# Earlier turns and first products of the next unit, and seven block products in another order

## The chip, the cores and the metric

The kernel runs on one core of a Trainium2 chip. What counts is the device time of one execution in microseconds; the times before are from ten runs. A core has TensorE (PE, with its weight loads PEld), VectorE (DVE), ScalarE (ACT), GpSimd (POOL) and SyncE (SP), which here issues the transfers. Each engine works through its own queue in the order of the program.

## The reference

A recurrent attention (RWKV-6) over 4 x 8 sequences of 768 tokens with 48 channels per head, and behind it a gated two-layer network.

```python
# attention: r, k, v, w are [4, 8, 768, 48], u is [8, 48]
for t in range(S):
    kt, vt, rt, wt = (k[:, :, t], v[:, :, t], r[:, :, t], w[:, :, t])
    cur = np.einsum('bhd,bhe->bhde', u[None] * kt, vt)
    y[:, :, t] = np.einsum('bhd,bhde->bhe', rt, state + cur)
    state = wt[:, :, :, None] * state + np.einsum('bhd,bhe->bhde', kt, vt)
# network: x = y as [3072, 384], w_in [384, 2048], w_out [2048, 384]
h = x @ w_in
g = h * (1.0 / (1.0 + np.exp(-h)))
out = g @ w_out
```

## The kernel before, in words

The work is cut into twelve units, numbered 0 to 11: a unit is a chunk of 128 tokens of two batches (256 tokens, 8 heads each). Units 0 and 1 load by tokens, units 2 to 11 by blocks of 32. For a unit the attention has these steps.

- `turn` (L360, VectorE) transposes the raw blocks of w, k and r, two instructions each. `product` (L408, GpSimd) builds a tree of products of the decays w, level by level, seven in all. `grow_own` multiplies keys (L634, GpSimd) and queries (L607, VectorE) by decays for levels 0 and 1; `odd_keys` (L595, ScalarE), `grow_keys` (L625, GpSimd), `grow_queries` (L607) and `prepare` (L737) go on with the higher levels.
- `burst` has TensorE compute the scores of two levels (L669), and `keep_level` writes them under a mask into the score tile (L679, VectorE).
- The blocks of eight tokens nearest to the diagonal are computed apart: `block_bonus` (L487, GpSimd, steps 0 to 7), `block_sum` (L521, VectorE, steps 0 to 4), `block_move` (two transfers through `kept`), `block_spread` (L548 to L551, ScalarE and one shuffle) and `block_write` (L557, VectorE).
- `turn_k` transposes the keys on TensorE (L781); `y_state`, `y` (L794, L807) give the output of the attention, `update` (L821, L826 on GpSimd, L835 on VectorE) the new state, and `move_x` sends the output to the network's layout (L857, SP).

The network follows one and two units behind. While `mix(i)` runs the attention of unit i, TensorE also does the eight `up` steps of unit i-1 (L924, each with a gate L933 on ScalarE) and the second layer of unit i-2. That second layer is a 2 x 2 block product in seven multiplications instead of eight (Winograd's form): `sums` (L972, VectorE) makes four combinations s1 to s4 of the gated values in `quarters` (part of `temps`), `weight_sums` (L964, once) makes t1, t2, t3 and a new b12 of the weights, and `quarter(i, which)` runs one of the seven products (L990) into one of two PSUM buffers `p_o`; ScalarE (L997) or VectorE (L999) combines and evicts it. This document counts the products from 0 in the order in which they run.

The order of everything is written out by hand (`manual_schedule`): `mix` returns thirteen groups of steps, and after each group `ROOM` says how many steps of the network follow:

```python
ROOM = 1, 1, 1, 2, 2, 1, 1, 1, 2, 1, 1, 1, 0
steps = downs(i - 2) + ups(i - 1)
```

So the seven products stand among groups 0 to 4 and the eight `up` steps among groups 5 to 11. Before the change, groups 0 to 2 hold the turns of unit i, all products of the tree and `grow_own`; the first block bonus of unit i+1 stands in group 10, and its sums 0 and 1 and bonus 4 and 5 at the end of group 12. A tile that is allocated again (`tk`, `tw` once, `tr` and `p_o` twice) waits for the last reader of the buffer it takes.

Of the kernel before, what the change touches and what calls it, by code (L numbers as in the profile page):

```python
# [15 lines left out]
ALU = mybir.AluOpType  # L16
# [22 lines left out]
def kernel(  # L39
# [11 lines left out]
    nc = tc.nc  # L51
# [4 lines left out]
    NL = 7  # L56
    NB = 2
# [8 lines left out]
    units = [(n, b0) for n in range(S // L) for b0 in range(0, B, NB)]  # L66
    NSLOT = 2
    NTOK = 2
    NPAIR = 3
# [75 lines left out]
    second = []  # L145
# [177 lines left out]
    first = {}  # L323
# [10 lines left out]
    for b in range(NB):  # L334
        for x in range(2):
            nc.vector.tensor_single_scalar(out=own_mask[:, b, :, x:x + 1], in_=first[0], scalar=tok[:, x, b:b + 1],
                                           op=ALU.is_equal)
# [113 lines left out]
    at = 768  # L451
# [94 lines left out]
    def block_spread(i):  # L546
        flat = block_both.rearrange("p b h s -> p b (h s)")
        nc.scalar.copy(out=flat[:, 0], in_=block_diag[0])  # L548
        for g in range(4):
            nc.scalar.copy(out=flat[(3 - g) * 32:(4 - g) * 32, 1], in_=block_diag[1][g * 32:(g + 1) * 32])  # L550
        nc.vector.stream_shuffle(out=flat[:, 1], in_=flat[:, 1], mask=list(range(31, -1, -1)))  # L551

    def block_write(i):

        shape = [128, NB, NP, L // BLK, BLK]
        for e in range(2):
            nc.vector.copy_predicated(out=score[:, i % NSC, e].rearrange("p (b q) (i s) -> p b q i s", b=NB, s=BLK),  # L557
                                      mask=block_mask[:, :, None].to_broadcast(shape),
                                      data=block_both[:, :, e::2][:, :, :, None, :].to_broadcast(shape))
# [301 lines left out]
    def both(fn, i, *args):  # L861
        return [(fn, i, b, *args) for b in range(NB)]
# [3 lines left out]

    def mix(i):

        early = i > NPAIR
        ahead = i + 1 < len(units)  # L870

        def bonus_steps(*steps):
            return [(block_bonus, i, x) for x in steps]

        def sum_steps(*steps):
            return [(block_sum, i, x) for x in steps]

        next_bonus = [(block_bonus, i + 1, x) for x in range(4)] if ahead else []
        next_sums = [(block_sum, i + 1, 0), (block_sum, i + 1, 1), (block_bonus, i + 1, 4), (block_bonus, i + 1, 5)] if ahead and early else []
        late = i == NPAIR + 1  # L880
        next_load = [(load_rk, i + 1)] if ahead else []
        move = [*sum_steps(3, 4), (block_move, i), *next_load]
        placed = [(block_spread, i), (block_write, i)]
        first = not early

        def at(now, *steps):
            return steps if now else ()

        groups = [[*both(turn, i, "w"), (product, i, 0)],
                  [*both(turn, i, "k"), *both(turn, i, "r"), (grow_own, i, 0)],  # L890
                  [*[(product, i, l) for l in range(1, NL)], (grow_own, i, 1), *at(late, *sum_steps(0, 1))],
                  [(odd_keys, i, 2), (grow_keys, i, 2, False), (grow_queries, i, 2), *at(early and not late, *sum_steps(2))],
                  [(prepare, i, 3), *at(first, *bonus_steps(2, 3), *sum_steps(0)), *at(late, *bonus_steps(4, 5)),
                   *at(early and not late, *bonus_steps(6, 7))],
                  [(burst, i, 3), (keep_level, i, 3), *at(first, *sum_steps(1), *bonus_steps(4, 5)),
                   *at(late, *sum_steps(2), *bonus_steps(6, 7)), *at(early and not late, *move)],
                  [(keep_level, i, 4), (go_on, i, 4), *at(first, (make_block_mask,), *sum_steps(2), *bonus_steps(6)), *at(late, *move)],
                  [(prepare, i, 5), (reverse_v, i), *at(first, *bonus_steps(7))],
                  [*at(first, *move), *at(early, *placed)],
                  [(burst, i, 5), (keep_level, i, 5), (keep_level, i, 6), (go_on, i, 6)],  # L900
                  [*at(first, *placed), *next_bonus],
                  both(turn_k, i) if i < len(units) - NB else [],
                  [*both(y_state, i), *both(y, i), *both(update, i), *next_sums, (move_x, i)]]

        loads = block_loads(i + NSLOT) if i + NSLOT < len(units) else []
        if i + 1 < len(units):
            loads.insert(len(loads) // 2, (load_values, i + 1))

        behind = groups[3 if i > NTOK + 1 else 10:]
        for at, group in enumerate(behind):  # L910
            group += loads[at * len(loads) // len(behind):(at + 1) * len(loads) // len(behind)]
        return groups
# [3 lines left out]
    FH, DH = FC // 2, DM // 2  # L916
# [46 lines left out]
        out, one, two = ((t1, b12, b11), (t2, b22, t1), (t3, b22, b12), (b12, b21, t2))[which]  # L963
        nc.vector.tensor_tensor(out=out, in0=one, in1=two, op=ALU.subtract)  # L964

    def sums(i, m):

        lower, upper = (gt[i, x].rearrange("p a (b t) -> p b a t", b=NB) for x in (m, m + FH // 2))
        s1, s2, s3, s4 = (quarters[:, x, 2 * m:2 * m + 2, :] for x in range(4))
        for out, one, two, op in ((s1, lower[:, 1], upper[:, 1], ALU.add), (s2, s1, lower[:, 0], ALU.subtract),  # L970
                                  (s3, lower[:, 0], lower[:, 1], ALU.subtract), (s4, upper[:, 0], s2, ALU.subtract)):
            nc.vector.tensor_tensor(out=out, in0=one, in1=two, op=op)  # L972

    ob, partial = {}, {}
# [1 line left out]
    def quarter(i, which):  # L976

        n, b0 = units[i]

        def g(b, half):  # L980
            return lambda f: gt[i, (f + half * FH) // 2][:, f % 2, b * L:(b + 1) * L]

        def s(x):
            return lambda f: quarters[:, x, f, :]

        p = second[0].tile([128, DH], F32, name="p_o", bufs=2)

        left, right = ((g(0, 0), b11), (g(0, 1), b21), (s(1), t2), (s(2), t3), (s(0), t1), (g(1, 1), b12), (s(3), b22))[which]
        for f in range(FH):
            nc.tensor.matmul(p, lhsT=left(f), rhs=right[:, f, :], start=(f == 0), stop=(f == FH - 1))  # L990
        if which == 0:
            ob[i] = [out_room(b) for b in range(NB)]
            partial[i] = pt.tile([128, 4, DH], F32, name="partial", bufs=1)
        c11, c12, c21, c22 = (ob[i][x][:, y * DH:(y + 1) * DH] for x in range(2) for y in range(2))
        u1, u2, u3, u4 = (partial[i][:, x, :] for x in range(4))
        if which == 0:
            nc.scalar.copy(out=u1, in_=p)  # L997
        for to, known in ((), ((c11, u1),), ((u2, u1),), ((u3, u2),), ((c22, u3), (u4, u2)), ((c21, u3),), ((c12, u4),))[which]:
            nc.vector.tensor_tensor(out=to, in0=p, in1=known, op=ALU.add)  # L999
        if which >= 5:  # L1000
            b = 6 - which
            row0 = (b0 + b) * S + n * L
            nc.sync.dma_start(out=out[row0:row0 + L, :], in_=ob[i][b])

    def ups(i):

        steps = [[(up, i, m)] for m in range(FC // 2)]
        for m in range(FH // 2 - 1):

            steps[FH // 2 + 1 + m].append((sums, i, m))  # L1010
        steps[-1].append((sums, i, FH // 2 - 1))
        return steps

    def downs(i):
        return [[(quarter, i, x)] for x in range(7)]

    def do(*steps):
        for fn, *args in steps:
            fn(*args)
# [16 lines left out]
    blocks = block_loads(2)  # L1036
# [37 lines left out]
    for m in range(6):  # L1074
# [3 lines left out]

    blocks = block_loads(4)
    do(*blocks[0:2], (level, 2, 2), (prepare, 2, 3), (weight_sums, 1), (down, 0, 1, 0), (down, 0, 0, 3), (down, 0, 1, 1),  # L1080
       (sums, 1, 0), (bonus, 2, 0), (bonus_sum, 2, 0))
    do(blocks[2], (burst, 2, 3), (keep_level, 2, 3), (keep_level, 2, 4), (go_on, 2, 4), (prepare, 2, 5), (bonus, 2, 1),
       (bonus, 2, 2), (down, 0, 1, 2), (bonus_sum, 2, 1), (load_rk, 3), (load_u,), (sums, 1, 1), *blocks[3:7], (down, 0, 1, 3))
    do((burst, 2, 5), (keep_level, 2, 5), (keep_level, 2, 6), (go_on, 2, 6), (up, 1, 6), (bonus_spread, 2), (bonus_write, 2),
       (load_values, 3), *both(turn_k, 2), (weight_sums, 2), (up, 1, 7), (sums, 1, 2))
    do((sums, 1, 3), *both(y_state, 2), *both(y, 2), *both(update, 2),
       (block_bonus, 3, 0), (block_bonus, 3, 1), (move_x, 2),
       *blocks[7:])

    ROOM = 1, 1, 1, 2, 2, 1, 1, 1, 2, 1, 1, 1, 0  # L1090
# [1 line left out]
    for i in range(3, len(units)):  # L1092
        steps = downs(i - 2) + ups(i - 1)
        groups = mix(i)
        if i == NTOK + 1:

            groups[3].insert(0, (weight_sums, 3))
        for group, room in zip(groups, ROOM):
            do(*group)
            for step in steps[:room]:  # L1100
                do(*step)
            steps = steps[room:]
# [32 lines left out]
```

## Time and profile before

| | |
|---|---|
| median of 10 runs | 636.53 us (635.84 to 637.32) |
| profiled execution, its own time | 638.04 us |
| its span | 636.3 us |
| TensorE busy | 621.5 us, 98% |
| VectorE busy | 438.7 us, 69% |
| GpSimd busy | 371.0 us, 58% |
| ScalarE busy | 185.4 us, 29% |
| granted TensorE clock, mean | 0.995 |

Busy time is the sum over instructions; a share near 100% means that the engine's queue is the limit, if its instructions are not themselves stretched. A line of a timeline holds the start and the length in us, the engine, the source line, the operation, the tiles written and read, the shape, how many such instructions follow each other, and in brackets the idle time of the engine just before and what ended it. The products of unit i-2 stand at the head of the stage of unit i: they start at 128.2 us for i = 3, 184.7 for i = 4, 235.8 for i = 5, then at 286.5, 335.2, 383.9, 432.7, 481.4 and 528.5 for i = 6 to 11.

### The profile page before, as it was taken

How to read it: one execution, taken by the hardware profiler on the slowest of the kernel's cores; microseconds unless marked ns; L12 is line 12 of the kernel's file. 1: busy time of each engine (PE TensorE's matmuls, PEld its weight loads, DVE VectorE, ACT ScalarE, POOL GpSimd, SP SyncE). 2: the span in 40 equal slices, each digit the busy share in tenths (PEclk: the TensorE clock that was granted, in tenths of full speed). 3: DMA queues.
4: the chain of work that ended last, by engine and by line, in shares of the span. 5: the costliest groups of instructions: out<-in, count | busy, mean ns of one | idle time of the engine just before them, and what ended most of it. 6: DMA issues, size and time to landing. Idle time of an engine off the chain costs nothing.

```text
span 636.3 us, 12245 instructions
## 1 busy us (share of the span) xinstructions
PE 621.5 (98%) x4574; PEld 563.7 (89%) x4574; DVE 438.7 (69%) x750; ACT 185.4 (29%) x377; POOL 371.0 (58%) x421
## 2 busy tenths in 40 slices
PE   8999999979998998999999999999999999999997
PEld 7878876869898898889889989989989989989997
DVE  7879779895696597587578488588578676561031
ACT  5798881200220320320320320320231221220120
POOL 6998297578369558657557657647747747600000
PEclk9999999988999999999999999999999999999999
DMA  9965854543343552643453552453353222100000
GB/s 229 286 178 134 196 163 50 113 75 66 77 73 55 98 95 51 126 62 52 97 77 51 111 75 50 92 92 53 72 104 54 43 67 51 35 0 26 26 1 25
DMA packets 203291, 53.75 MB, mean 84 GB/s; under 512 B 186464, under 2 KB 194656, under 8 KB 203232
## 3 DMA queue, kind: packets, MB, share of 16 engines
q1 hardware_dynamic: 201648, 52.39, 40.4%
q10 hardware_dynamic: 1584, 0.59, 0.4%
q8 instruction: 36, 0.59, 0.4%
q14 instruction: 23, 0.19, 0.1%
HBM read 43.67 MB, written 5.31 MB: 77 GB/s over the span
## 4 chain that ended last, share of the span: by engine, by line
PE 79%; SPq 6%; DVE 5%; DMA 5%; POOL 2%; issue 2%; ACT 1%; POOLq 0%; DVEq 0%; ACTq 0%
PE p_h L924 31%; PE p_o L990 29%; PE p_sc L669 5%; SPq L109 4%; DMA tokens_w<-in_w_dram 3%; PE p_m L946 2%; PE p_m L807 2%; PE p_m L669 2%; PE p_m L794 2%; PE p_m L372 2%; POOL tk L625 1%; DVE score L679 1%; PE p_m L1025 1%; PE p_m L781 1%; DVE tw L360 1%
## 5 line engine op out<-in xcount | busy, mean ns | idle before, releaser
L924 PE MATMUL p_h<-xt,w_in_sb 128*128 128x256 f32 x1152 | 258.1, 382 | 0.7 <-DVE xt L847 0.7
L924 PEld LDWEIGHTS p_h<-xt,w_in_sb 128*128 128x128 f32 x1152 | 215.9, 190 | 32.6 <-POOL tk L649 0.9
L933 ACT ACTIVATE gt<-p_h 128x512 f32<-128x512 f32 x90 | 53.6, 597 | 227.6 <-PE p_h L924 227.5
L625 POOL TENSOR_TENSOR tk<-tk,tw 128x256 f32<-128x256 f32 x126 | 86.9, 711 | 33.8 <-ACT tk L595 14.6
L990 PE MATMUL p_o<-own,temps 128*128 128x192 f32 x528 | 91.2, 333 | 8.3 <-DVE temps L999 8.3
L990 PEld LDWEIGHTS p_o<-own,temps 128*128 128x128 f32 x528 | 88.8, 195 | 9.2 <-DVE temps L999 9.2
L487 POOL TENSOR_TENSOR ruk<-tokens_rk 128x768 f32<-128x768 f32 (+1 forms) x36 | 51.9, 1453 | 71.8 <-DVE block_sums L521 31.8
L990 PE MATMUL p_o<-w_out_sb,gt 128*128 128x192 f32 x508 | 87.3, 328 | 0.0
L990 PEld LDWEIGHTS p_o<-w_out_sb,gt 128*128 128x128 f32 x508 | 82.6, 190 | 0.9 <-issue 0.4
L972 DVE TENSOR_TENSOR temps<-gt 128x256 f32<-128x256 f32 x84 | 51.7, 615 | 28.7 <-ACT gt L933 28.6
L607 DVE TENSOR_TENSOR tr<-tr,tw 128x512 f32<-128x512 f32 x62 | 51.7, 834 | 13.1 <-POOL tw L408 10.0
L595 ACT COPY tk<-tk 128x256 f32<-128x256 f32 x51 | 20.5, 402 | 127.2 <-POOL tk L634 103.6
L408 POOL TENSOR_TENSOR tw<-tw 128x256 f32<-128x256 f32 (+6 forms) x83 | 47.6, 573 | 14.1 <-DVE tw L360 10.2
L679 DVE COPY_PREDICATED score<-mask,p_sc 128x512 f32<-128x512 int8 x60 | 42.1, 756 | 15.2 <-PE p_sc L669 14.4
L826 POOL TENSOR_TENSOR state<-state,tw 128x512 f32<-128x512 f32 x16 | 19.9, 1263 | 41.4 <-PE p_m L794 41.4
L669 PEld LDWEIGHTS p_sc<-tr,tk 48*128 48x128 f32 x496 | 30.4, 187 | 10.2 <-issue 6.3
L669 PE MATMUL p_sc<-tr,tk 48*128 48x128 f32 x496 | 36.5, 285 | 0.8 <-POOL tk L625 0.6
L557 DVE COPY_PREDICATED score<-spare 128x1024 f32<-128x1024 int8 x18 | 32.9, 1882 | 0.3
L999 DVE TENSOR_TENSOR temps<-p_o,partial 128x192 f32<-128x192 f32 x22 | 7.9, 358 | 36.0 <-PE p_o L990 25.8
L634 POOL TENSOR_TENSOR tk<-tk,tw 128x256 f32<-128x256 f32 x36 | 31.2, 888 | 0.0
L990 PE MATMUL p_o<-w_out_sb,temps 128*128 128x192 f32 x176 | 30.4, 326 | 0.0
L990 PEld LDWEIGHTS p_o<-w_out_sb,temps 128*128 128x128 f32 x176 | 28.9, 190 | 0.0
(170 smaller groups left out, 809.7 us busy)
## 6 DMA issues: line engine op xcount, KB each, us to landing
w_out_sb<-in_moe_w_in_dram SPq DMA_DIRECT2D x6, 768.0 KB, 6.7
tokens_rk<-in_r_dram SPq DMA_DIRECT2D x9, 384.0 KB, 4.4
tokens_rk<-in_k_dram SPq DMA_DIRECT2D x9, 384.0 KB, 5.3
tokens_w<-in_w_dram SPq DMA_DIRECT2D x9, 384.0 KB, 6.4
w_out_sb<-in_moe_w_out_dram SPq DMA_DIRECT2D x4, 768.0 KB, 6.7
own<-in_moe_w_out_dram SPq DMA_DIRECT2D x4, 768.0 KB, 6.2
xt<-yt SPq DMA_DIRECT2D x60, 48.0 KB, 2.0
raw<-in_w_dram SPq DMA_DIRECT2D x80, 32.0 KB, 2.2
```

The lines of the kernel that those rows point to most:

```text
L408: engine.tensor_tensor(out=up, in0=t[:, :, 0::2], in1=t[:, :, 1::2], op=ALU.mult)
L487: mul = lambda out, one, two: nc.gpsimd.tensor_tensor(out=out, in0=one, in1=two, op=ALU.mult)
L557: nc.vector.copy_predicated(out=score[:, i % NSC, e].rearrange("p (b q) (i s) -> p b q i s", b=NB, s=BLK), mask=block_mask[:, :, None].to_ ...
L607: nc.vector.tensor_tensor(out=odd, in0=odd, in1=tw[i][l][:, :, 0::2][:, :, :, None].to_broadcast([128, Q, L >> (l + 1), c]), op=ALU.mult)
L625: nc.gpsimd.tensor_tensor(out=out, in0=have, in1=odd_products(i, l, b, *blocks), op=ALU.mult)
L634: nc.gpsimd.tensor_tensor(out=have, in0=have, in1=odd_products(i, l, b, [2, NP * ni]), op=ALU.mult)
L669: nc.tensor.matmul(bass.AP(tensor=s_p.tensor, offset=s_p.offset, ap=[s_p.ap[0], [apart * L // 2, 2], [1, L // 2]]), lhsT=tk[i][rows, X[l % ...
L679: nc.vector.copy_predicated(out=dst, mask=masks[l][:, :, None].to_broadcast([128, NB, NP, ni, c]), data=sc[e].rearrange("p (b q) (i c) -> ...
L924: nc.tensor.matmul(p_h[:, a, :], lhsT=w_in_sb[:, c, f * 128:(f + 1) * 128], rhs=xt[i][:, c, :], start=(c == 0), stop=(c == KC - 1))
L933: nc.scalar.activation(out=gt[i, m], in_=p_h, func=AF.Silu)
L972: nc.vector.tensor_tensor(out=out, in0=one, in1=two, op=op)
L990: nc.tensor.matmul(p, lhsT=left(f), rhs=right[:, f, :], start=(f == 0), stop=(f == FH - 1))
```

## The change

It has three parts. First, from unit 4 on the turns, the tree and `grow_own` of unit i+1 are issued at the end of unit i: the turns, the first product of the tree and `grow_own` of level 0 between `turn_k` and `y_state`, the rest behind `update`. Unit 3, the first to run in `mix`, keeps them at its head. Secondly, the block steps of units 3, 4 and 5 stand at other places: unit 3 does its bonus steps 0 to 3 in group 4, unit 4's bonus steps 0 to 3 stand at the end of unit 3 and its sums 0 and 1 and bonus 4 and 5 in group 2, and the last shuffle of `block_spread` goes into `block_write`. Thirdly, the seven products run in another order, and s4 and s3 are computed between them: s4 behind product 1, s3 behind product 2. `weight_sums(2)` moves into group 2 of unit 3, `weight_sums(3)` to the end of its group 3.

```diff
 def block_spread(i):
...
-        nc.vector.stream_shuffle(out=flat[:, 1], in_=flat[:, 1], mask=list(range(31, -1, -1)))
 def block_write(i):
+        flat = block_both.rearrange("p b h s -> p b (h s)")
+        nc.vector.stream_shuffle(out=flat[:, 1], in_=flat[:, 1], mask=list(range(31, -1, -1)))
 def mix(i):
-        groups = [[*both(turn, i, "w"), (product, i, 0)],
-                  [*both(turn, i, "k"), *both(turn, i, "r"), (grow_own, i, 0)],
-                  [*[(product, i, l) for l in range(1, NL)], (grow_own, i, 1), *at(late, *sum_steps(0, 1))],
...
-                  both(turn_k, i) if i < len(units) - NB else [],
-                  [*both(y_state, i), *both(y, i), *both(update, i), *next_sums, (move_x, i)]]
+        def turns(j):
+            return [*both(turn, j, "w"), (product, j, 0), *both(turn, j, "k"), *both(turn, j, "r"), (grow_own, j, 0)]
+        def start(j):
+            return [*[(product, j, l) for l in range(1, NL)], (grow_own, j, 1)]
+        early = bonus_steps(i + 1, 0, 1, 2, 3)
+        middle = [*sum_steps(i + 1, 0, 1), *bonus_steps(i + 1, 4, 5)]
+        move = [*sum_steps(i, 3, 4), (block_move, i), *at(ahead, (load_rk, i + 1))]
+        groups = [[*at(first, *both(turn, i, "w"), (product, i, 0))],
+                  [*at(first, *both(turn, i, "k"), *both(turn, i, "r"), (grow_own, i, 0))],
+                  [*at(first, *start(i)), *at(second, *sum_steps(i, 0, 1), *bonus_steps(i, 4, 5))],
+                  [(odd_keys, i, 2), (grow_keys, i, 2, False), (grow_queries, i, 2), *at(later, *sum_steps(i, 2))],
+                  [(prepare, i, 3), *at(first, *bonus_steps(i, 0, 1, 2, 3)), *at(later, *bonus_steps(i, 6, 7))],
...
+                  [*at(later and ahead, *early), *at(first, (block_write, i))],
+                  [*at(i < len(units) - NB, *both(turn_k, i)), *at(ahead, *turns(i + 1))],
+                  [*both(y_state, i), *both(y, i), *both(update, i), *at(ahead, *start(i + 1)), *at(first, *early),
+                   *at(later and ahead, *middle), (move_x, i)]]
-    def sums(i, m):
+    def sums(i, m, part):
-        for out, one, two, op in ((s1, lower[:, 1], upper[:, 1], ALU.add), (s2, s1, lower[:, 0], ALU.subtract),
-                                  (s3, lower[:, 0], lower[:, 1], ALU.subtract), (s4, upper[:, 0], s2, ALU.subtract)):
+        steps = ((s1, lower[:, 1], upper[:, 1], ALU.add), (s2, s1, lower[:, 0], ALU.subtract),
+                 (s4, upper[:, 0], s2, ALU.subtract), (s3, lower[:, 0], lower[:, 1], ALU.subtract))
+        for out, one, two, op in (steps[0:2], steps[2:3], steps[3:4])[part]:
             nc.vector.tensor_tensor(out=out, in0=one, in1=two, op=op)
 def quarter(i, which):
-        left, right = ((g(0, 0), b11), (g(0, 1), b21), (s(1), t2), (s(2), t3), (s(0), t1), (g(1, 1), b12), (s(3), b22))[which]
+        left, right = ((g(0, 0), b11), (g(0, 1), b21), (s(1), t2), (s(0), t1), (s(3), b22), (s(2), t3), (g(1, 1), b12))[which]
-        for to, known in ((), ((c11, u1),), ((u2, u1),), ((u3, u2),), ((c22, u3), (u4, u2)), ((c21, u3),), ((c12, u4),))[which]:
+        for to, known in ((), ((c11, u1),), ((u2, u1),), ((u4, u2),), ((c12, u4),), ((u3, u2), (c22, u4)), ((c21, u3),))[which]:
-        if which >= 5:
-            b = 6 - which
+        if which in (4, 6):
+            b = which // 2 - 2
 def downs(i):
-        return [[(quarter, i, x)] for x in range(7)]
+        steps = [[(quarter, i, x)] for x in range(7)]
+        for part in 1, 2:
+            steps[part] += [(sums, i, m, part) for m in range(FH // 2)]
+        return steps
...
-       (load_values, 3), *both(turn_k, 2), (weight_sums, 2), (up, 1, 7), (sums, 1, 2))
-    do((sums, 1, 3), *both(y_state, 2), *both(y, 2), *both(update, 2),
-       (block_bonus, 3, 0), (block_bonus, 3, 1), (move_x, 2),
+       (load_values, 3), *both(turn_k, 2), (up, 1, 7), (sums, 1, 2, 0))
+    do((sums, 1, 3, 0), *both(y_state, 2), *both(y, 2), *both(update, 2),
+       (move_x, 2),
...
-            groups[3].insert(0, (weight_sums, 3))
+            groups[2].append((weight_sums, 2))
+            groups[3].append((weight_sums, 3))
```

## The prediction, made before the changed kernel ran

> **What bounds the kernel now.** I read the page's busy shares, then TensorE's waits, then the timelines of TensorE, VectorE and GpSimd around each wait.
>
> ```profile
> PE 621.5 (98%) x4574; PEld 563.7 (89%) x4574; DVE 438.7 (69%) x750; ACT 185.4 (29%) x377; POOL 371.0 (58%) x421
> ```
> ```profile
> PE p_o L990 <- DVE temps L999: 8.3, 3, 4.7
> ```
> ```profile
> 140.98 8.25 PE L990 MATMUL p_o<-own,temps 128*128 128x192 f32 x32 [4.67 <-DVE temps L999]
> ...
> 194.86 5.47 PE L990 MATMUL p_o<-own,temps 128*128 128x192 f32 x32 [2.08 <-DVE temps L999]
> ...
> 245.47 5.47 PE L990 MATMUL p_o<-own,temps 128*128 128x192 f32 x32 [1.60 <-DVE temps L999]
> ```
>
> TensorE works nearly without a break; its order is the time. What it loses inside the loop is three waits in the stages of units 3, 4 and 5, all of one kind. The seven block products (counted from 0) rotate through two PSUM buffers `p_o`, so product 3 needs product 1 evicted (L999), and that eviction stands in VectorE's queue behind the sums and the turns (L360). From unit 6 on there is no such wait: a stage takes 48.7 us, all TensorE. The first wait costs more than its 4.67 us, because the clock drops behind it:
>
> ```profile
> 142.00:143.00 1.00, 1.00 (x4) 1.00 (x4) 1.00 (x1) 0.00 (x0) 1.00 (x1) 0.50 0.35 97
> ...
> 147.00:148.00 1.00, 1.00 (x8) 1.00 (x7) 0.00 (x0) 0.00 (x0) 1.00 (x2) 1.00 0.38 46
> ```
>
> The column after POOL is the granted clock: 0.50, then 1.00. 32 matmuls took 8.25 us there against 5.47 later, a loss of 2.78. In all, 4.67 + 2.78 + 2.08 + 1.60 = 11.1 us could be had; the rest of TensorE's 14.8 idle us is the start and the tail.
>
> **How close the later units are to the same wait.** Unit 8, VectorE's and then TensorE's timeline:
>
> ```profile
> 395.35 1.12 DVE L521 TENSOR_REDUCE block_sums<-ruk 128x4 f32<-128x192 f32 x4
> 396.39 0.35 DVE L999 TENSOR_TENSOR partial<-p_o,partial 128x192 f32<-128x192 f32 x1
> ```
> ```profile
> 397.00 2.76 PE L990 MATMUL p_o<-w_out_sb,gt 128*128 128x192 f32 x16
> ```
>
> That product starts 0.26 us after the eviction ends: no slack worth the name. And VectorE's adds are not always 0.42 us (VectorE, then GpSimd):
>
> ```profile
> 380.25 0.42 DVE L972 TENSOR_TENSOR temps<-gt 128x256 f32<-128x256 f32 x1 [1.91 <-ACT gt L933]
> 380.71 1.17 DVE L972 TENSOR_TENSOR temps<-temps,gt 128x256 f32<-128x256 f32 x1
> 381.80 1.26 DVE L972 TENSOR_TENSOR temps<-gt 128x256 f32<-128x256 f32 x1
> 382.98 0.41 DVE L972 TENSOR_TENSOR temps<-gt,temps 128x256 f32<-128x256 f32 x1
> ```
> ```profile
> 380.56 2.22 POOL L826 TENSOR_TENSOR state<-state,tw 128x512 f32<-128x512 f32 x2 [6.67 <-PE p_m L794]
> ```
>
> While GpSimd's two products run, the adds and the products take turns: an add lasts one GpSimd product plus its own time.
>
> [...] The lines above agree, and so do L521 and L999 (at most one SBUF input), which keep 0.34 to 0.36 us whatever GpSimd does. [...] 4.67 us brought 0.50, the waits of 2.08 and 1.60 none. [...] I use start-to-start spacings there (0.6 us for small L487 and L625 products).
>
> **The change, part by part.** No matmul is added or removed. (a) `sums` computes s1 and s2 early as before, but s4 (4 adds) now stands behind the eviction of product 1 and s3 (4 adds) behind that of product 2. (b) The products come as s2, s1, s4, s3, b12, so product 4 needs s4 and product 5 needs s3 and the eviction of product 3. (c) From unit 4 on, the turns (6 L360, 3.8 us), the first query product (L607) and, on GpSimd, the first tree product and L634 stand ahead of `y_state`; tree products 2 to 7, the second L634 pair and bonus steps 4 and 5 directly behind `update`. Turning k still waits for TensorE's transposes of the old k (375.95 to 376.99), so it lands about 8 us ahead of the stage, 10 us earlier than now. (d) Unit 3's bonus steps 0 and 1 (1.98 and 1.88 us) leave the stretch before its stage; `weight_sums(2)` (2.59 us) moves from ahead of its turns to behind product 1; unit 4's bonus steps 0 to 3 go to the end of unit 3; unit 3's `block_spread` copies move up ahead of one gate on ScalarE, which is idle 71%: zero, at most the 2 us that `kept` needs to land. (e) SP: output rows leave at products 4 and 6 instead of 5 and 6, `block_move(4)` is issued before four raw loads of 0.5 us each. Neither queue ends on the path: the raw slots are loaded a unit ahead. If that cover were gone, turns wait up to the 2 us that a raw load takes to land. Zero for (e), and zero for the tail: product 6, one eviction, one output transfer, GpSimd idle there.
>
> **Walking a steady unit (6 to 10).** Times count from product 0 (383.90 in unit 8); a product takes 2.65 us, so product 1 ends at 5.3, product 5 is due at 13.1. GpSimd cannot start its part before the state products, tied to `y_state` at -3.3: 2 L826, 6 L408 (2.4), 2 L634 (1.5), and the four adds that interleave bring it to 4.3; then bonus 4 and 5 (2 of 1.0, 4 of 0.6), 4 L625 (0.65 each), bonus 6 (1.8). So it is busy through the whole of 5.3 to 13. VectorE between the end of product 1 and product 5: semaphore 0.2, three evictions 1.1, eight adds at 0.36 start to start 2.9, L607 0.66, four reductions L521 1.1: 6.0 of 7.8 us, slack 1.8. But nine of these have two SBUF inputs. In strict turns: s4 waits 0.44 + 3 x 0.6, s3 waits 0.25 + 2 x 0.65 (one falls into GpSimd's wait for ScalarE's copy L595), L607 0.65: 4.4 us with nothing else in the way. That is 2.6 us over the slack: behind the waiting adds stand L607, L521 and the eviction of product 3 in VectorE's queue, for that eviction waits product 5, and behind it on TensorE product 6 and the score burst. TensorE has no slack, so it loses the 2.6 in every unit. Strict turns are the dearer end (0 is the cheaper, no meeting at all); if one add more slips through a gap between dependent GpSimd products (0.6), it is 2.0. I take 2.0: 5 x 2.0 = 10.0.
>
> **Unit 5** likewise: 2.0 in place of 1.60, +0.4. **Unit 11** has no state product before it, GpSimd is three us earlier and only bonus 6 is in the way: +0.9, between 0 and 1.4.
>
> **Unit 4** has unit 4's bonus 0 to 3 (1.9, 1.85, 1.0, 1.1) in GpSimd's queue where s4 stands: four waits of that length put the eviction of product 2, behind s4 and two L521 (1.5), 3.9 us past product 4's due time; s3 against bonus 4 and 5 then adds 3.7. With 0.9 off for gaps 6.7, less the old 2.08: +4.6.
>
> **Unit 3** keeps its turns where they were. Freed of L964 and four sums, product 1 is evicted at about 134.7, before product 3 is due (136.2): the 4.67 goes. What is late next: s4, L607 and `weight_sums(2)` in front of the eviction of product 2 (+1.95), then s3, L607 and `weight_sums(3)` (1.74 and its wait) in front of that of product 3 (+4.55). 6.5 in place of 4.67, and a gap of 4.5 us costs the clock loss again: +1.8.
>
> Sum: 10.0 + 0.4 + 0.9 + 4.6 + 1.8 = +17.7. The profiled execution took 638.04 (span 636.3, 1.7 around it), 1.5 above the median of the ten; a difference carries over: 636.5 + 17.7 = 654.2.
>
> **Rivals.** *The cover holds.* If VectorE and GpSimd don't meet in this stretch (waits under the 1.8 of slack), unit 3's evictions come at 134.3, 138.5 and 142.7, each before it is due, and all 11.1 us are won: 625.4. For it: VectorE is idle 31%, and turning early is right for units 4 and 5. Against: GpSimd's queue, tied to -3.3, has 12 us of work. *Half.* With 2.7 us of lock waits the steady loss is 0.8: 5 x 0.8 - 0.8 (unit 5) + 2 (unit 4) - 3 (unit 3) = +2.2, 638.7. *GpSimd ends it.* VectorE's adds also delay GpSimd by 9 x 0.36; unit 4's L625 reach 20 and its burst is due at 18.4; with two further clock losses (2 x 2.8) and dearer steady waits (3.0): about 666. *It doesn't do what it says*: the program's order shows turns and adds at their new places, so this can only be the wait of turn k on the transposes, which is counted.
>
> **Chances.** Slower by the walk (645 to 662) 0.60, half 0.18 (0.14 of it slower, 0.04 even), GpSimd 0.06: slower 0.80 in all; within 0.2% (1.3 us, about what a measurement tells from none) 0.04; faster 0.16. The range leaves out the fast case and the worst tail: 635 to 666; the likeliest alone 645 to 662.
>
> **What would show it.** Right: TensorE waits for L1002 (the new number of L999) of about 2 us in each of units 5 to 10, before the product with s3; sums in the stage at 0.9 to 1.3 us each; stages of 50 to 51 us from unit 6. Wrong: stages of 48.7 us and sums at 0.42 (the cover holds), or waits at L669 for GpSimd (the third rival).

## The result and the profile after

The changed kernel takes 654.21 us (median of 8 runs, 651.78 to 656.01) against 636.63 for the kernel before on the same chip (28 runs): ratio 1.0274, 95% interval 1.0263 to 1.0286. It is 2.7% slower. The profiled execution took 653.81 us, its span is 652.0 us, the mean granted clock 0.989.

First the page's busy shares of the changed kernel, then the list of TensorE's waits (us in total, times, longest). L1002 is the old L999, the eviction of a block product by VectorE; the other lines have moved by 2 or 3.

```profile
PE 626.9 (96%) x4574; PEld 566.8 (87%) x4574; DVE 469.2 (72%) x750; ACT 186.1 (29%) x377; POOL 377.4 (58%) x421
```
```profile
PE p_o L993 <- DVE partial L1002: 18.0, 9, 3.2
...
PE p_h L926 <- ACT gt L935: 0.8, 1, 0.8
```

The counts of instructions are the old ones on every engine. VectorE is busy 30.5 us longer with the same 750 instructions: they are stretched. TensorE's span less its busy time is 25.1 us instead of 14.8, and its busy time has itself grown by 5.4 us. TensorE's timeline shows where:

```profile
144.13 2.87 PE L993 MATMUL p_o<-own,temps 128*128 128x192 f32 x16 [2.77 <-DVE partial L1002]
...
194.79 5.49 PE L993 MATMUL p_o<-w_out_sb,temps 128*128 128x192 f32 x16 [3.18 <-DVE partial L1002]
...
250.78 2.87 PE L993 MATMUL p_o<-own,temps 128*128 128x192 f32 x16 [1.31 <-DVE partial L1002]
...
301.75 4.35 PE L993 MATMUL p_o<-own,temps 128*128 128x192 f32 x16 [1.96 <-DVE partial L1002]
...
405.38 2.87 PE L993 MATMUL p_o<-own,temps 128*128 128x192 f32 x16 [1.96 <-DVE partial L1002]
...
557.33 2.87 PE L993 MATMUL p_o<-own,temps 128*128 128x192 f32 x16 [0.91 <-DVE partial L1002]
```

The waits in units 7, 9 and 10, left out here, are 1.96 too. All but that of unit 4 stand before product 5, the one with s3. One of them in detail, unit 8, VectorE's timeline and then GpSimd's:

```profile
395.71 0.36 DVE L1002 TENSOR_TENSOR temps<-p_o,partial 128x192 f32<-128x192 f32 x1 [2.22 <-issue]
395.99 2.62 DVE L975 TENSOR_TENSOR temps<-gt,temps 128x256 f32<-128x256 f32 x4
398.53 0.34 DVE L1002 TENSOR_TENSOR partial<-p_o,partial 128x192 f32<-128x192 f32 x1
398.80 2.99 DVE L975 TENSOR_TENSOR temps<-gt 128x256 f32<-128x256 f32 x4
401.71 2.31 DVE L609 TENSOR_TENSOR tr<-tr,tw 128x512 f32<-128x512 f32 x1
403.94 1.12 DVE L521 TENSOR_REDUCE block_sums<-ruk 128x4 f32<-128x192 f32 x4
404.99 0.34 DVE L1002 TENSOR_TENSOR partial<-p_o,partial 128x192 f32<-128x192 f32 x1
```
```profile
396.02 2.31 POOL L487 TENSOR_TENSOR tokens_rk<-tokens_rk,tokens_w 128x192 f32<-128x192 f32 x3
398.29 3.22 POOL L627 TENSOR_TENSOR tk<-tk,tw 128x256 f32<-128x256 f32 x4
401.47 2.01 POOL L487 TENSOR_TENSOR spare<-tokens_rk 128x768 f32<-128x768 f32 x1
```

The three L1002 are the evictions of products 1, 2 and 3. Between the second and the third stand four s3, one L609 and four L521. In this profile the instructions with at most one SBUF input keep their length (an L1002 lasts 0.34 to 0.36 us, one of these short L521 0.33 to 0.35, beside GpSimd and alone); those with two (L975, L609) last about as long as the GpSimd instructions beside them: an add of s3 0.75 us beside an L627 of 0.80, L609 2.31 beside an L487 of 2.01. One by one, the four L627 end at 399.14, 399.94, 400.73 and 401.50, and 0.28 to 0.29 us behind each of these ends an s3; "taking turns" stands for this below. TensorE starts product 5 at 405.38, just behind the third eviction.

Last, the clock, in stretches of 1 us from the span's start (the column after POOL's is the granted clock):

```profile
303.00:304.00 1.00, 1.00 (x5) 1.00 (x5) 0.88 (x1) 0.00 (x0) 0.34 (x1) 0.50 0.69 216
...
355.00:356.00 1.00, 1.00 (x8) 1.00 (x8) 1.00 (x1) 0.00 (x0) 0.98 (x1) 1.00 0.48 121
...
457.00:458.00 1.00, 1.00 (x5) 1.00 (x5) 1.00 (x1) 0.00 (x0) 0.93 (x1) 0.50 0.42 122
```

In units 6 and 9 the clock is halved behind the wait of 1.96, in unit 7 (355) it isn't, behind a wait of the same length. The last section shows how the two differ.

The stages in the two profiles, by the starts of product 0 (us):

| unit | before | after | difference |
|---|---|---|---|
| up to 3 | 128.24 | 127.88 | -0.36 |
| 3 | 56.47 | 53.06 | -3.41 |
| 4 | 51.09 | 55.27 | +4.18 |
| 5 | 50.61 | 50.31 | -0.30 |
| 6, 9 | 48.74 | 52.66 | +3.92 each |
| 7, 8 | 48.75 | 50.97 | +2.22 each |
| 10 | 47.15 | 49.37 | +2.22 |
| 11 and tail | 107.72 | 108.88 | +1.16 |

Together +15.8, the difference of the spans (636.26 and 652.03 with two decimals). The profiled execution of before is 1.4 above its median, that of after 0.4 below, so the medians lie 17.6 apart.

### The profile page after: what moved, and what is told of

It reads as the page before. It is cut to its first block, busy times and chain, and to the rows that moved or that the text cites. A ratio compares the mean times of both kernels' runs of the same rounds, so it can differ in the third digit from the quotient of the medians.

```text
span 652.0 us, 12253 instructions
## 1 busy us (share of the span) xinstructions
PE 626.9 (96%) x4574; PEld 566.8 (87%) x4574; DVE 469.2 (72%) x750; ACT 186.1 (29%) x377; POOL 377.4 (58%) x421
## 4 chain that ended last, share of the span: by engine, by line
PE 68%; DVE 18%; POOL 4%; issue 4%; DMA 3%; ACT 1%; SPq 1%; DVEq 0%; POOLq 0%; ACTq 0%
PE p_h L926 35%; PE p_o L993 16%; DVE temps L975 7%; PE p_sc L671 4%; DVE tr L609 4%; DVE block_sums L521 3%; PE p_m L809 3%; PE p_m L796 2%; PE p_m L948 2%; PE p_m L671 2%; POOL tk L627 1%; DMA tokens_w<-in_w_dram 1%; DVE partial L1002 1%; DMA raw<-in_r_dram 1%; PE p_m L783 1%
## 5 line engine op out<-in xcount | busy, mean ns | idle before, releaser
L627 POOL TENSOR_TENSOR tk<-tk,tw 128x256 f32<-128x256 f32 x126 | 93.0, 758 | 79.6 <-PE p_sc L671 40.8
L935 ACT ACTIVATE gt<-p_h 128x512 f32<-128x512 f32 x90 | 53.5, 596 | 260.2 <-PE p_h L926 260.0
L993 PE MATMUL p_o<-own,temps 128*128 128x192 f32 x528 | 93.6, 336 | 14.9 <-DVE partial L1002 14.8
L487 POOL TENSOR_TENSOR ruk<-tokens_rk 128x768 f32<-128x768 f32 (+1 forms) x36 | 53.5, 1497 | 41.3 <-DMA tokens_rk<-in_k_dram 27.9
L975 DVE TENSOR_TENSOR temps<-gt 128x256 f32<-128x256 f32 x84 | 59.2, 735 | 22.2 <-ACT gt L935 22.2
L408 POOL TENSOR_TENSOR tw<-tw 128x256 f32<-128x256 f32 (+6 forms) x83 | 41.7, 502 | 38.9 <-DVE tw L360 35.0
L609 DVE TENSOR_TENSOR tr<-tr,tw 128x512 f32<-128x512 f32 x62 | 57.3, 924 | 3.7 <-POOL tk L627 1.1
L993 PE MATMUL p_o<-w_out_sb,temps 128*128 128x192 f32 x176 | 33.2, 346 | 3.2 <-DVE partial L1002 3.2
L993 PEld LDWEIGHTS p_o<-w_out_sb,temps 128*128 128x128 f32 x176 | 31.2, 203 | 3.7 <-DVE partial L1002 3.7
L636 POOL TENSOR_TENSOR tk<-tk,tw 128x256 f32<-128x256 f32 x36 | 32.8, 931 | 0.5
L487 POOL TENSOR_TENSOR tokens_rk<-tokens_rk,tokens_w 128x192 f32<-128x192 f32 (+1 forms) x36 | 31.1, 883 | 1.4
L559 DVE COPY_PREDICATED score<-spare 128x1024 f32<-128x1024 int8 x18 | 30.6, 1750 | 0.3
L1002 DVE TENSOR_TENSOR temps<-p_o,partial 128x192 f32<-128x192 f32 x22 | 7.9, 358 | 31.7 <-PE p_o L993 15.8
```

The costliest lines, as they stand in the source:

```text
L408: engine.tensor_tensor(out=up, in0=t[:, :, 0::2], in1=t[:, :, 1::2], op=ALU.mult)
L487: mul = lambda out, one, two: nc.gpsimd.tensor_tensor(out=out, in0=one, in1=two, op=ALU.mult)
L609: nc.vector.tensor_tensor(out=odd, in0=odd, in1=tw[i][l][:, :, 0::2][:, :, :, None].to_broadcast([128, Q, L >> (l + 1), c]), op=ALU.mult)
L627: nc.gpsimd.tensor_tensor(out=out, in0=have, in1=odd_products(i, l, b, *blocks), op=ALU.mult)
L636: nc.gpsimd.tensor_tensor(out=have, in0=have, in1=odd_products(i, l, b, [2, NP * ni]), op=ALU.mult)
L935: nc.scalar.activation(out=gt[i, m], in_=p_h, func=AF.Silu)
```

## The experiments

The theory: the eviction of product 3 comes late because, in that stretch, VectorE's instructions with two SBUF inputs take turns with GpSimd's. Rivals: VectorE's queue is simply too long or wrongly ordered there, whatever GpSimd does; the early turns make the loss; the new order of the products makes it. In some of these kernels the lines are one or two below those of the changed kernel (L1000 and L1001 are then its L1002).

### Turns alone, and products alone

The kernel in which the turns, tree products and bonus steps have their new places, but `sums`, `quarter`, `downs` and `weight_sums` are those of before:

```diff
     def downs(i):
-        steps = [[(quarter, i, x)] for x in range(7)]
-        for part in 1, 2:
-            steps[part] += [(sums, i, m, part) for m in range(FH // 2)]
-        return steps
+        return [[(quarter, i, x)] for x in range(7)]
...
-            groups[2].append((weight_sums, 2))
-            groups[3].append((weight_sums, 3))
+            groups[3].insert(0, (weight_sums, 3))
```

> The new places of turns, query products, tree products and bonus steps, but all four sums early (as before), the seven products in the old order, weight_sums at the old places. Theory (the sums in the stage, taking turns with GpSimd, make the loss): no sums stand in the stage, so no wait from unit 6 on; the old waits of units 4 and 5 (2.08 and 1.60 us) go, since the turns no longer stand in front of product 1's eviction; unit 3 as before or better. About 632 us, 627 to 637. Rival (turning early itself makes it[...]): waits of about 2 us stay in units 6 to 10, 648 or more.

Measured: 637.65 us against 636.76, ratio 1.0008 (0.9997 to 1.0020): no difference. From unit 6 on TensorE has no wait, as the theory said, and the rival falls. The 632 was too low: the first units have waits again, only elsewhere.

```profile
PE p_o L992 <- DVE temps L1001: 4.5, 3, 2.8
PE p_o L992 <- DVE partial L1001: 2.1, 1, 2.1
```

The longest, 2.75 in unit 5, is for product 1's eviction: unit 4's own score path is late (its shuffle L555, ahead of L559, could begin only at 218.05, after 8.3 us in which VectorE waited for ScalarE's copies L550), and behind it sums, turns and the state L837 all come late in VectorE's queue. There it is 10.4 us from product 0's start to the eviction, in unit 8 only 5.8.

The opposite half, the new product order and the split sums in the kernel before:

> The new product order and the split sums alone, with turns, query products, bonus steps and weight_sums at the old places. Theory: the turns (3.8 us of VectorE) and the eight sums now share the stretch in front of the eviction of product 3; by VectorE's own durations 2.0 us over the slack in each unit from 6 to 10, with turn-taking 3 to 5: 652 to 668 us, slower than the full change. Rival (early turns make the loss): no new wait, 636 to 638. Rival (plain queue length, no turn-taking): 2.0 in each unit, about 650.

Measured: 654.84 us, ratio 1.0285 (1.0265 to 1.0306). The loss is all there without an early turn. TensorE in unit 8:

```profile
403.32 2.87 PE L991 MATMUL p_o<-w_out_sb,temps 128*128 128x192 f32 x16 [1.65 <-DVE partial L1000]
407.18 2.87 PE L991 MATMUL p_o<-own,temps 128*128 128x192 f32 x16 [0.99 <-DVE partial L1000]
```

Two waits, 2.6 us together, instead of one of 1.96, and stages of 51.92 us instead of 50.97. So with the sums in the stage the early turns help by about 1 us in a unit. But none of the waits of 1.65 brought a slow clock (the mean is 0.997), as two of those of 1.96 did, and in the total the two kernels come out level. Between turn-taking and mere length of the queue this run doesn't decide: 2.6 lies between the 2.0 expected of length alone and the 3 to 5 expected with turn-taking.

### The order of the products, without the split

The changed kernel with its new product order, all four sums early and the old places of `weight_sums`:

> The changed kernel with the new product order, but all four sums computed early and the weight_sums at the old places. Theory (the split of the sums, not the order of the products, makes the loss): no wait before product 5 from unit 6 on; the waits of the first units as with the turns alone; 636 to 639 us. Rival (the new order needs its evictions sooner): waits of 1 us or more in units 6 to 10, 643 or more.

Measured: 636.96 against 636.62, ratio 1.0012 (0.9999 to 1.0025), no wait from unit 6 on. The order costs nothing; what costs are eight adds in the stage.

### GpSimd's work taken away

```diff
-            return [(block_bonus, j, x) for x in steps]
+            return [(block_bonus, j, x) for x in steps if j < NPAIR + 2 or x not in (4, 5, 6)]
```

> The changed kernel with GpSimd's bonus steps 4, 5 and 6 left out from unit 5 on (their part of the result is missing). Theory (VectorE's sums and L609 take turns with these GpSimd products): the sums fall back to about 0.4 us each, except beside L627; the waits of 1.96 us before product 5 in units 6 to 10, the 1.31 of unit 5 and the 0.91 of unit 11 go, and with them the slow-clock products behind two of them: 654.2 - 9.8 - 1.3 - 0.9 - 3.3 = about 639 us. Rival (plain length and order of VectorE's queue): VectorE has the same instructions, so the waits stay, 652 to 655.

Measured: 637.33 us, ratio to before 1.0009 (1.0000 to 1.0017); against the changed kernel 16.9 us less. VectorE's queue is the same, instruction for instruction, so its length or order alone is not the cause. Unit 8, VectorE and GpSimd:

```profile
389.91 1.90 DVE L975 TENSOR_TENSOR temps<-gt,temps 128x256 f32<-128x256 f32 x4
392.18 0.36 DVE L1002 TENSOR_TENSOR partial<-p_o,partial 128x192 f32<-128x192 f32 x1 [0.37 <-PE p_o L993]
392.45 1.42 DVE L975 TENSOR_TENSOR temps<-gt 128x256 f32<-128x256 f32 x4
393.79 0.68 DVE L609 TENSOR_TENSOR tr<-tr,tw 128x512 f32<-128x512 f32 x1
...
395.43 0.34 DVE L1002 TENSOR_TENSOR partial<-p_o,partial 128x192 f32<-128x192 f32 x1
```
```profile
387.90 2.62 POOL L627 TENSOR_TENSOR tk<-tk,tw 128x256 f32<-128x256 f32 x4 [0.52 <-ACT tk L597]
395.59 1.82 POOL L487 TENSOR_TENSOR ruk<-tokens_rk 128x768 f32<-128x768 f32 x1 [5.07 <-DVE block_sums L521]
```

Where GpSimd is idle, four sums take 1.42 us and L609 0.68; in the changed kernel 2.62, 2.99 and 2.31. That prices the turn-taking in the steady stage: 1.2 for s4, 1.6 for s3, 1.6 for L609, 4.4 us in all.

Do these add up, or does one of them decide? Two kernels each take away a part. First step 6 alone (`x != 6` in the line above):

> The changed kernel with GpSimd's bonus step 6 alone left out from unit 5 on (its part of the result is missing), steps 4 and 5 kept. In the changed kernel, unit 8, four s4 took 2.62 us, four s3 2.99 and L609 2.31, where the kernel with steps 4, 5 and 6 left out showed 1.42 for four sums and 0.68 for L609: 1.2, 1.6 and 1.6 us of turn-taking. Theory (they add up, slack about 2.4): without step 6 L609 takes 0.7, so the wait of 1.96 before product 5 in units 6 to 10 is about 0.3: 654.2 - 8.3 - 3.3 (clock) - 1.3 = about 641 us, 638 to 645. Rival (the sums alone make the wait): 650 or more.

Measured: 643.49 against 636.11, ratio 1.0114 (1.0085 to 1.0142). VectorE, then TensorE, in unit 8:

```profile
392.60 2.62 DVE L975 TENSOR_TENSOR temps<-gt,temps 128x256 f32<-128x256 f32 x4
...
395.42 2.99 DVE L975 TENSOR_TENSOR temps<-gt 128x256 f32<-128x256 f32 x4
398.32 0.68 DVE L609 TENSOR_TENSOR tr<-tr,tw 128x512 f32<-128x512 f32 x1
```
```profile
400.36 2.87 PE L993 MATMUL p_o<-own,temps 128*128 128x192 f32 x16 [0.33 <-DVE partial L1002]
```

The sums are as they were, L609 is 1.63 shorter, and so is TensorE's wait: 0.33 for 1.96. Then steps 4 and 5 alone:

> The changed kernel with GpSimd's bonus steps 4 and 5 left out from unit 5 on, step 6 kept (that part of the result is missing). Theory: GpSimd is some 4.5 us earlier, its L627 meet s4 (as in the kernel with all three left out, 1.9 us) and step 6 meets one or two of s3 (+1 to 2 us), L609 is alone: the wait before product 5 in units 6 to 10 is 0 to 0.6, 638 to 643 us. Rival (step 6 alone decides, wherever it stands): the wait stays at 1.5 or more, 648 or more.

Measured: 638.40, ratio 1.0037 (1.0026 to 1.0049), no wait before product 5 from unit 6 on. Step 6 still meets somebody:

```profile
388.80 3.52 DVE L975 TENSOR_TENSOR temps<-gt,temps 128x256 f32<-128x256 f32 x4
...
392.52 1.41 DVE L975 TENSOR_TENSOR temps<-gt 128x256 f32<-128x256 f32 x4
```

Four s4 take 3.52 now (L627 and step 6 beside them), yet s3 and L609 are free, and the sum stays inside the slack. The three parts add, and it is the sum against the slack that decides.

A first try to take step 6 out of the way had failed. It issued steps 6 and 7 behind the burst of level 3:

> The changed kernel with GpSimd's bonus steps 6 and 7 issued behind the burst of level 3 instead of behind prepare, nothing left out. The 2.31 us of L609 (0.66 alone) stood beside bonus step 6. Theory in its present form (four waits for s4, two for s3 and that one for L609 add up): L609 takes about 0.7, the wait before product 5 in units 6 to 10 falls from 1.96 to about 0.35: 654.2 - 8.0 - 3.3 (clock) - 1.3 = about 642 us, 640 to 646. Rival (the sums alone, as the prediction's walk had it, with 0.65 for L609 beside L627): little changes, 650 to 655.

Measured: 652.40, ratio 1.0258 (1.0239 to 1.0277), and the waits of 1.94 to 1.96 as before. The trace tells why: step 6 stands where it stood, right behind L627 (it starts at 401.67, the four L627 last from 398.48 to 401.70), because GpSimd's own queue holds nothing between the old place and the new one: issued later, it did not start later. So this run says nothing on step 6; the one without it does.

### The same work behind the eviction

Nothing left out; L609 of level 2 and the four L521 stand behind products 3 and 4 (in unit 3 L609 keeps its place):

```diff
-                  [(odd_keys, i, 2), (grow_keys, i, 2, False), (grow_queries, i, 2), *at(later, *sum_steps(i, 2))],
-                  [(prepare, i, 3), *at(first, *bonus_steps(i, 0, 1, 2, 3)), *at(later, *bonus_steps(i, 6, 7))],
+                  [(odd_keys, i, 2), (grow_keys, i, 2, False), *at(first, (grow_queries, i, 2))],
+                  [*at(later, (grow_queries, i, 2), *sum_steps(i, 2)), (prepare, i, 3), *at(first, *bonus_steps(i, 0, 1, 2, 3)), *at(later, *bonus_steps(i, 6, 7))],
```

> The changed kernel with the query product L609 of level 2 and, from unit 4 on, the four reductions L521 behind products 3 and 4 instead of in front of product 3's eviction. Theory (that eviction comes late in VectorE's queue): it comes 2.31 + 1.12 = 3.4 us earlier, product 5 has no wait in units 5 to 11: 654.2 - 9.8 - 1.3 - 0.9 - 3.3 = about 639 us, 637 to 645 if some of it comes back as a wait before the score burst. Rival (product 5 waits for its sums s3 or for weights, not for the eviction): unchanged, 653 to 656.

Measured: 637.03, ratio 1.0006 (0.9995 to 1.0018): all of the 17.6 us come back. Unit 8, VectorE, then TensorE:

```profile
387.94 2.62 DVE L975 TENSOR_TENSOR temps<-gt,temps 128x256 f32<-128x256 f32 x4
390.49 0.34 DVE L1002 TENSOR_TENSOR partial<-p_o,partial 128x192 f32<-128x192 f32 x1
390.75 2.98 DVE L975 TENSOR_TENSOR temps<-gt 128x256 f32<-128x256 f32 x4
393.66 0.35 DVE L1002 TENSOR_TENSOR partial<-p_o,partial 128x192 f32<-128x192 f32 x1
```
```profile
395.20 2.76 PE L993 MATMUL p_o<-own,temps 128*128 128x192 f32 x16
```

The sums still take turns (2.62 and 2.98), but the eviction ends 1.2 us before product 5 starts, and from unit 6 on TensorE has no wait and the clock stays up. The adds' waits are not dear in themselves; they were dear because of what stood behind them in VectorE's queue.

### A version that beats both

Left over are unit 3 (2.77) and unit 4 (3.2 and a slow clock behind it). The next kernel adds three moves: L609 of level 2 behind products 3 and 4 in unit 3 too, `weight_sums(3)` to the same place, and unit 4's bonus steps 0 to 3 ahead of `turn_k`, where the later units have them.

```diff
-                  [*at(later and ahead, *early), *at(first, (block_write, i))],
+                  [*at(first, (block_write, i)), *at(ahead, *early)],
...
-            groups[3].append((weight_sums, 3))
+            groups[4].insert(0, (weight_sums, 3))
```

The lines that move L609 are those above without the exception for unit 3.

> Query product L609 of level 2 and the L521 of the stage behind products 3 and 4 in every unit, unit 3 too; weight_sums(3) moved behind products 3 and 4 as well; bonus steps 0 to 3 of unit 4 ahead of the old keys' transposes (as for later units) instead of behind unit 4's start. Theory: this takes the wait of unit 3 (2.77), that of unit 4 (3.18 and 2.73 of slow clock) and keeps units 5 to 11 free of waits: 637.0 - 2.8 - 5.9 = about 628.5 us, 626 to 634, faster than the kernel before. Rival (a wait moves on: product 6 of unit 3 waits for weight_sums(3), or the unit 4 score path is late): 634 to 638.

Measured: 633.97 against 636.62, ratio 0.9957 (0.9944 to 0.9971): 0.4% faster than the kernel before, 3% faster than the changed one. The wait of unit 3 is gone and the clock is 1.000. The 628.5 was missed by 5.5: in units 4 and 5 new, shorter waits appear (five over 0.5 us, 4.96 together). The next kernel has them too; GpSimd, VectorE and TensorE in unit 4:

> The same with unit 3's block_spread (ScalarE) back behind the last score products, as in the kernel before. Theory: the wait for ScalarE's gate at L935 in unit 3's stage (0.80 us in the changed kernel) is due to block_spread standing ahead of that gate: it goes, 0.2 to 0.8 us faster than the kernel with all the other edits. Rival (the gate was late for another reason): no difference.

```profile
173.47 1.90 POOL L487 TENSOR_TENSOR ruk<-tokens_rk 128x768 f32<-128x768 f32 x1 [8.82 <-DMA tokens_rk<-in_k_dram]
```
```profile
185.02 1.12 DVE L837 TENSOR_TENSOR state<-p_sc,state 48x384 f32<-48x384 f32 x2 [1.93 <-POOL state L828]
...
186.99 0.36 DVE L1002 TENSOR_TENSOR temps<-p_o,partial 128x192 f32<-128x192 f32 x1
```
```profile
187.40 2.87 PE L993 MATMUL p_o<-own,temps 128*128 128x192 f32 x16 [2.25 <-DVE temps L1002]
```

Bonus step 0 waits for its tokens from memory until 173.47; four bonus steps, a tree product and two L636 then stand ahead of the state products L828 in GpSimd's queue, VectorE waits 1.93 for these, and behind L837 stands the eviction of product 1. The cost has moved to another wait and shrunk on the way.

The last kernel's own question was ScalarE's gate: measured 633.69, ratio 0.9953 (0.9941 to 0.9966), 0.3 us from the kernel without the edit, less than the intervals resolve. The wait for L935 in unit 3's stage (0.62 in the one) is gone from the list of the other, so `block_spread` ahead of the gate did make it; but the wait before product 3 of unit 4 grew from 1.49 to 2.25 in its place, and nothing is gained: TensorE reaches product 0 of that stage 1.0 us earlier (177.09 for 178.11), but the eviction of product 1 begins only 0.26 earlier (186.99 for 187.25).

## Why the prediction was right, and where it was not

The time was foretold as 654.2 and is 654.21. The direction and the cause were right; that the number is so close is luck. Two terms were wrong by 5.2 and 3.4 us, in opposite directions, and the largest one came out right by errors that cancel.

**The steady units: the mechanism right, the size by cancelling errors.** 2.0 was taken for each of the units 6 to 10; measured are 1.96 in each, before product 5, for L1002, and stages longer by 2.22. That sums are longer beside GpSimd, on which it rests, is borne out by four s3 that take 2.99 in the changed kernel and 1.42 where GpSimd is idle. But the walk's strict turns were an estimate, and the meetings were priced wrongly. It let an add wait for a whole GpSimd product of 0.6 and then take its own 0.36; in the trace an add in turn with GpSimd lasts about as long as the stretched product beside it, 0.75, so that a meeting costs 0.4. (The adds of 1.17 and 1.26 beside products of 1.1 already said as much.) That made s4 1.2 (walked 2.2). s3 met L627 four times and not two to three times, 1.6 (walked 1.55), and L609 met bonus step 6 instead of an L627, 1.6 (walked 0.65). The sum is 4.4 in both. The sign "sums in the stage at 0.9 to 1.3 us each" did not come: they took 0.66 and 0.75. The slack was larger than the 1.8 of the walk: 4.4 less the wait of 1.96 leaves 2.4, and so do the 2.8 that remain without step 6, less 0.33. The 0.6 that was taken off for gaps between GpSimd's products happened to be what was missing from the slack.

**The clock behind a short wait: wrong.** From "4.67 us brought 0.50, the waits of 2.08 and 1.60 none" the prediction went by the length of a wait, and put the clock behind the steady waits of 2 us at nothing. In the steady units it was halved behind two of five waits of 1.96 (1.7 us of each of these two stages), which is +3.4 in this profile. The length alone does not tell these apart, but where the wait falls does (last section): the 2.08 of the kernel before lay across two of the clock's steps of 3.41 us, with 1.68 and 0.40. The mean clocks of the eight executions of the changed kernel, 0.986 to 0.995, show that the number of such drops differs between them. It is part of their scatter of 4.2 us, not all of it: the three at 0.995 alone lie 2.3 apart.

**Unit 3: wrong sign.** +1.8 was foretold, -3.4 measured. The step that failed first is "s4, L607 and `weight_sums(2)` in front of the eviction of product 2 (+1.95)". Four s4 took 1.88 there and L966 1.75, so that the eviction began at 138.10, in time for product 4, which had no wait; GpSimd's products beside them were short (L408, 0.56 each), and the adds lost only 0.5 to them. One wait remained, 2.77 before product 5 instead of 4.55, with L966 (2.21) and L609 (1.15) in front of the eviction. And the clock, which was to cost 2.8 again, did not fall behind it in this execution. Waits of 2.77 for 6.5 and no clock loss for 2.8 make -6.5; 0.8 of the other 1.3 is the gate of the next paragraph, the rest is not traced.

**Unit 3, the copies moved ahead of a gate: inside the bound.** "Zero, at most the 2 us that `kept` needs to land": 0.80, TensorE waiting for the gate L935 behind `block_spread`.

**Unit 4: right sum, other parts.** +4.6 foretold, +4.18 measured. The wait before product 4 is 3.18 (walked 3.9): four s4 took 5.62 us beside bonus steps 0 to 3. The second, 3.7 before product 5, did not come, as product 4 itself ran at half speed, 5.49 us for 2.76, and hid it. Where the clock came back sooner (the kernel without step 6, whose unit 4 is the same), product 4 took 4.53 and a wait of 1.07 stood before product 5. So the clock took what the second wait was to take, and the close sum is luck again.

**Units 5 and 11 and the rest: right within a microsecond.** Unit 5 -0.3 (foretold +0.4; the wait is 1.31, not 2.0), unit 11 +1.2 with a wait of 0.91 (foretold +0.9), and from product 0 of unit 10 on the tail takes 60.5 us, as before (60.6).

Sum of the misses: unit 3 -5.2, clock +3.4, steady units +1.1, unit 5 -0.7, unit 4 -0.4, unit 11 +0.3, start -0.4: -1.9, which is 15.8 less 17.7. The distance of the two profiled executions to their medians gives 1.8 us back.

**The rivals.** *The cover holds* is refuted by the waits. The kernel that comes nearest to it, with GpSimd's part left out from unit 5 on, still took 637.33 and not 625.4, since waits of 2.77 and 3.19 in units 3 and 4, both with a slow clock, remained. *Half* needed waits on GpSimd of 2.7; they are 4.4, against a slack of 2.4. *GpSimd ends it* didn't come: the bursts did not wait longer than before.

## What to carry to other kernels

In the steady stage of the changed kernel VectorE's instructions with two SBUF inputs lasted about as long as the GpSimd instruction beside them (an add of s3 0.75 us for 0.36, L609 2.31 for 0.68). Where a trace shows the same, count them so, add the waits that this makes along VectorE's queue and set them against the slack of the next thing that TensorE needs from that queue. Before taking work out of such a stretch, look at what can go behind the needed eviction: here the same instructions two products later gave all of the loss back. Before issuing a step later, look whether its engine's own queue holds something between: bonus step 6 had nothing there, and started right behind L627 as before (401.67, against 401.47 in the changed kernel).

## What the runs showed of the hardware

Behind waits of TensorE of the same length, 1.96 us, the clock was halved in units 6 and 9 of the changed kernel and not in units 7, 8 and 10. In its profile and in that of the kernel before, all changes of the granted clock lie whole multiples of 3.41 us apart (before: at 139.85 and 146.67 us; changed: at 193.74, 200.57, 302.97, 306.38, 456.57, 459.98 and 651.13), and each of the four drops that end before the program does lasts one or two such steps, 3.41 or 6.83 us. The twelve waits before a block product in these two profiles can be laid against the steps. In four of them 1.96 us or more fell within one step (3.41 of the 4.67 in the kernel before, and the three halved waits of the table), and each time the clock was halved at the end of that step. In the other eight at most 1.95 us fell within one step, and it was not.

| wait of the changed kernel | its parts in the steps it touches (us) | clock |
|---|---|---|
| unit 3, 2.77 | 1.18, 1.59 | full |
| unit 4, 3.18 | 2.13, 1.05 | halved |
| units 6 and 9, 1.96 | 1.96 | halved |
| unit 7, 1.96 | 1.72, 0.24 | full |
| unit 8, 1.96 | 1.95, 0.01 | full |
| unit 10, 1.96 | 0.73, 1.23 | full |

By length alone it looks like chance: over the twelve profiles, of the waits before a block product up to 1.66 us none of 45 was followed by a halved clock, of those from 1.85 to 2.77 us 7 of 25, and of those of 2.93 us and more 8 of 8. A drop made the products behind it 1.7 to 2.8 us longer (unit 6 of the changed kernel: 4.35 and 3.00 us for 2.87 and 2.76; unit 3 of the kernel before: 8.25 for 5.47). The parts within a step are those of twelve waits in two profiles; that another kernel's clock goes by the same 1.96 us is not shown.
